# One kernel for attention and two expert layers: GpSimd's work in the seven-product stage given to VectorE, the cosine's argument folded once, half of the cosines computed in the output stage

## The chip, the cores and the metric

The kernel runs on one core of a Trainium2 chip. A core has five engines that run their own instruction streams: TensorE (PE, matmuls), VectorE (DVE), ScalarE (ACT), GpSimd (POOL) and SyncE (SP, which here issues the DMAs). The metric is device time of one execution, in microseconds (us); lower is better. The kernel before the change took 1310.09 us, the median of three runs (1306.05 to 1311.13).

## The reference, cut to what matters

Attention over 4 batches, 8 heads, 576 tokens, head size 64, which keeps the 32 largest scores of a row; then a gated layer on the 2304 tokens; then a second layer with a cosine in it, which the change is about.

```python
def _moe_ref(x, w_gate, w_val, w_out):            # 512 -> 1536 -> 512
    g = x @ w_gate
    silu = g * (1.0 / (1.0 + np.exp(-g)))
    return (silu * (x @ w_val) @ w_out)

def _moe2_ref(x, w_in, w_out):                    # 512 -> 2048 -> 512
    h = x @ w_in
    g = h * np.cos(h)
    return (g @ w_out)
```

All inputs and the output are float32. The kernel works in a reduced float32 form of TensorE: where it needs the full precision, an operand is split into a high half (a copy by ACT into the reduced type) and a low half (the difference, a `tensor_sub`), and three matmuls are summed: high by high, low by high, high by low.

## The kernel before, in words

The 2304 tokens are 18 tiles of 128. Attention runs in units of one tile and one head; the first layer runs beside it in ten chunks (`SIZES`, two chunks of one tile and eight of two). `gemm_proc` computes gate and value of a chunk, 12 steps of 128 hidden columns; `wout_proc` multiplies by the output weights; `y_proc` turns the result and stores it to DRAM (`y1`). The last chunk comes when attention is done: its PSUM banks are three of a new pool (`psB`, banks 0 to 2), and its gated product (`silu`, `product`, L937 and L940) and its low half (L966) are made by DVE.

The second layer's first matmul (hidden 2048) is computed in Strassen's manner, seven products in place of eight. It has 4 groups of 576 tokens (`NCB`) and, for each, 8 pairs of 128-column hidden blocks (`NPR`), in all 32 pairs; a pair makes two rows, of 128 x 576. For each token group `x2_proc` loads four blocks of `y1`, forms four differences (POOL, L1352) and splits the seven operands into high half (ACT, L1369) and low half (DVE, L1373). For each two pairs `win_proc` does the same with the weights, once: four sums and differences (POOL, L1268), seven high halves (ACT, L1284), seven low halves (L1288, DVE for five, POOL for two). A weight set goes into tiles that the last chunk's weights have left; the last of its four sets waits for that chunk's end. `h_proc` runs a pair: seven steps of six matmuls (L1402) on three PSUM banks, between them three copies to SBUF by ACT (L1433, L1489 and one more) and four additions or copies from PSUM by DVE (L1446, L1467, L1474, L1480), on which the next steps wait. The first `ALONE` pairs use banks 3, 4 and 5 one after the other, the next ones up to `BOTH` alternate between banks 0 to 2 and 3 to 5, later ones go around all eight.

`row_proc` takes each of the 64 rows h. It divides by two pi and rounds to a whole number of turns (ACT, L1538, into int32), subtracts the turns from h in two steps with a two-part constant (DVE, L1545 and L1549), takes the absolute value and the sine (ACT, L1552, L1554), multiplies by h (POOL, L1555) and stores the row to DRAM (`gd`). A ring of three tiles holds the rows of either side until then.

The output stage (`piece_proc`, `o_proc`) loads `gd` in 72 pieces of 128 tokens x 512 hidden columns (tile t, quarter m of 4), splits each into halves (ACT L1626, DVE L1630) and runs 12 matmuls per piece (L1653). `wout2_proc` prepares the 16 weight tiles (ACT L1584, POOL L1587). The first four tiles go quarter by quarter (`AHEAD`), the others tile by tile. A loaded piece is in one of five tiles (tag xr), a split one in one of seven (tag xc), which the last pair's operands share.

The order of the instructions on each engine is fixed when the program is built: every step is a generator's item with an engine, a cost and a due time, and `Plan.run` gives each engine, as it comes free, the ready item with the earliest due time. At run time an engine executes its list strictly in order and waits on semaphores. Three lines show the form of an item:

```python
yield "DVE", 0.67, rest, due, True                  # engine, cost in us, what to issue, due time, depends
item = min((x for x in queue if x[0] <= t), key=lambda x: x[1:3])
self.free[engine] = end
```

Of the kernel before, what the change touches and what calls it, by code (L numbers as in the profile page):

```python
# [40 lines left out]
CB = S  # L41
NCB = NTOK // CB
NLAST = 3
ALONE = 3
BOTH = 6
AHEAD = 4
WLEAD = 20.0
HALF = S // 2
SCALE = 1.0 / math.sqrt(D)
STEEP = 2.0 ** 96  # L50
LOWEST = -3.0e38
INV2PI = 1.0 / (2.0 * math.pi)
C1 = 6.28125
C2 = 2.0 * math.pi - C1
SIGN = -2 ** 31
NK = 10
NQ = 3
# [108 lines left out]
def topk_attention_moe_moe(ctx: ExitStack, tc: tile.TileContext, qT, kT, vP, w1, wo1, w2, out):  # L166
# [672 lines left out]
    r_y = [Ring(1) for _ in range(NYB)]  # L839
    ev_g = {(c, f): Event() for c in range(NCH) for f in range(NF1)}  # L840
    ev_gemm = {(c, f): Event() for c in range(NCH) for f in range(NF1)}
    ev_tanh = Event()
    r_o = [Ring(1) for _ in range(4)]
    steps = [NF1 // 2 if turned else NF1 for turned in TURNED]
    K0 = [sum(steps[:c]) for c in range(NCH + 1)]
# [41 lines left out]
    def gemm_proc(c, f):  # L887
# [5 lines left out]
        yield ev_w1[f]  # L893
        last = c == NCH - 1
        if last:
            yield ev_pb
        n = SIZES[c] * 128
        gv, done = {}, [Event(), Event()]

# [26 lines left out]
        if last:  # L926
            done[1].set(end + plan.LAT["PE"], plan)
            yield done[0]
            yield done[1]
            yield r_vv.gate(k)  # L930
            th = TH.pop(k)
            if f == NF1 - 1:
                ev_tanh.set(done[0].time, plan)

            def silu():
                VV[k] = wide("vv", n)
                nc.vector.scalar_tensor_tensor(VV[k], th, 1.0, gv[0], op0=OP.add, op1=OP.mult)  # L937

            def product():
                nc.vector.scalar_tensor_tensor(VV[k], VV[k], 0.5, gv[1], op0=OP.mult, op1=OP.mult)  # L940

            end = yield "DVE", 0.36, silu, due, True
            rings[0][0].free(rings[0][1], end, plan)
            r_th.free(k, end, plan)
            end = yield "DVE", 0.36, product, due, True
            rings[1][0].free(rings[1][1], end, plan)
            vv = VV[k]
        else:
            for g in range(2):
# [13 lines left out]

        yield "ACT", 0.07 + 0.00092 * n, hi, due, True
        eng, name, cost = (nc.vector, "DVE", 0.33) if last else (nc.gpsimd, "POOL", 0.05 + 0.0025 * n)
        end = yield name, cost, lambda: eng.tensor_sub(G[c, f][1], vv, G[c, f][0]), due, True  # L966
        r_vv.free(k, end, plan)
        ev_g[c, f].set(end, plan)

# [115 lines left out]
            r_x.free(2 + c, end, plan)  # L1085

    def y_proc(c, i):
        due = moe_due(c, NF1)
        bank = yt[i % NYB]
        y4 = bank.rearrange("p (f n) -> p f n", f=KT)  # L1090
        for half in range(2):
            ko = yo_count[0]
            yo_count[0] += 1
            yield r_yo.gate(ko)
            y2 = y4[:, 2 * half:2 * half + 2]
            st = {}
# [25 lines left out]
    HN = CB // 2  # L1122
    NPR = NF2 // 2
    SEVEN = 7
    ev_pb, ev_pbx, ev_ph = Event(), Event(), Event()
    X2, W2I, W2O = {}, {}, {}
    ev_w2 = {(q, m): Event() for q in range(NF2 // 4) for m in range(SEVEN)}
    ev_x2 = {(j, m): Event() for j in range(NCB) for m in range(SEVEN)}
# [1 line left out]
    ev_gd = [Event(NF2) for _ in range(NCB)]  # L1130
    r_xc, r_wr, r_xr = Ring(SEVEN), Ring(5), Ring(5)
    r_ha, r_hb2, r_k2, r_r2 = Ring(3), Ring(3), Ring(2), Ring(4)
    ev_rows = {n: Event() for n in range(NCB * NF2)}
# [15 lines left out]
    def pool_b_proc():  # L1149
# [7 lines left out]
            opened("psB", space=PSUM, side="right", reuse_waits="tile")  # L1157

        t = yield "-", 0.0, swap, 0.0, True
        ev_pb.set(t, plan)  # L1160
        for f in range(NF1):
            yield ev_gemm[NCH - 1, f]
# [61 lines left out]
    def win_proc(q):  # L1224
# [32 lines left out]
        def add(m, x, y, op, first, wait=()):  # L1257
            yield have[x]
            yield have[y]
            for e in wait:  # L1260
                yield e

            def fn():
                if m == "S3":
                    alloc(m)
                else:
                    tiles[m] = tiles[first]
                nc.gpsimd.tensor_tensor(tiles[m], tiles[x], tiles[y], op=op)  # L1268

            t = yield "POOL", 1.3, fn, due + W_ORDER.index(m), True  # L1270
            made(m, t)
            done(x, t)
            done(y, t)

        def split(n, m):
# [8 lines left out]
                nc.scalar.activation(w[:, 0], tiles[m], AF.Copy)  # L1284

            yield "ACT", 0.52, hi, d, True
            eng, name, cost = (nc.gpsimd, "POOL", 1.25) if n % 3 == 2 else (nc.vector, "DVE", 0.75)
            t = yield name, cost, lambda: eng.tensor_sub(W2I[q, n][:, 1], tiles[m], W2I[q, n][:, 0]), d, True  # L1288
            done(m, t)
            ev_w2[q, n].set(t, plan)  # L1290

# [17 lines left out]
    def x2_proc(j):  # L1309
# [29 lines left out]
        def add(m, x, y, first, wait=()):  # L1339
# [7 lines left out]
            def fn():  # L1347
                if m in ("T1", "T2"):
                    alloc(m)
                else:  # L1350
                    tiles[m] = tiles[first]
                nc.gpsimd.tensor_sub(tiles[m], tiles[x], tiles[y])  # L1352

            t = yield "POOL", 1.5, fn, due - 12.0, True
            have[m].set(t, plan)
            done(x, t)
            done(y, t)
# [1 line left out]
        def split(n, m):  # L1359
# [7 lines left out]
            def hi():  # L1367
# [2 lines left out]

            t = yield "ACT", 0.6, hi, due + n * 0.5, True
            ev_xh[j, n].set(t, plan)
            t = yield ("DVE", 0.8, lambda: nc.vector.tensor_sub(X2[j, n][:, 1], tiles[m], X2[j, n][:, 0]),  # L1373
                       due + n * 0.5, True)
            done(m, t)
            ev_x2[j, n].set(t, plan)
# [143 lines left out]
    r_s1, r_s2, r_s3 = Ring(2), Ring(1), Ring(1)  # L1520
    ev_wfree = {(q, n): Event() for q in range(NF2 // 4) for n in range(SEVEN)}

    def row_proc(k, side, rows, ready):
        n = 2 * k + side
        j, f = divmod(n, NF2)
        due = b_due(k) + 8.0 + side
        yield ready
        if n:
            yield ev_rows[n - 1]
        yield ev_pbx  # L1530
        yield r_k2.gate(n)
        yield r_r2.gate(n)
        h = rows[side]
        st = {}

        def turns():
            st["k"] = pools["pbx"].tile([128, CB], I32, tag="k", name="k", bufs=r_k2.n)
            nc.scalar.activation(st["k"], h, AF.Copy, scale=INV2PI)  # L1538

        t = yield "ACT", 0.6, turns, due, True  # L1540
        ev_rows[n].set(t, plan)

        def rest():
            r = st["r"] = pools["pbx"].tile([128, CB], F32, tag="r", name="r", bufs=r_r2.n)
            nc.vector.scalar_tensor_tensor(r, st["k"], -C1, h, op0=OP.mult, op1=OP.add)  # L1545

        yield "DVE", 0.67, rest, due, True
        r = st["r"]
        t = yield ("DVE", 0.67, lambda: nc.vector.scalar_tensor_tensor(r, st["k"], -C2, r, op0=OP.mult, op1=OP.add),  # L1549
                   due, True)  # L1550
        r_k2.free(n, t, plan)
        yield "ACT", 0.6, lambda: nc.scalar.activation(r, r, AF.Abs), due, True  # L1552
        yield ev_tanh
        yield "ACT", 0.6, lambda: nc.scalar.activation(r, r, AF.Sin, scale=-1.0, bias=halfpi), due, True  # L1554
        t = yield "POOL", 1.5, lambda: nc.gpsimd.tensor_mul(r, r, h), due, True  # L1555
        (r_ha, r_hb2)[side].free(k, t, plan)
        t = yield "DMA", 1.2, lambda: nc.sync.dma_start(gd[:, f, j * CB:j * CB + CB], r), due, True
        r_r2.free(n, t, plan)
        ev_gd[j].set(t, plan)

    def o_due(n):
# [2 lines left out]
    def wout2_proc(f):  # L1564
# [19 lines left out]
            nc.scalar.activation(W2O[f][:, 0], st["x"], AF.Copy)  # L1584

        yield "ACT", 0.52, hi, due + 3.0, True
        t = yield ("POOL", 1.25, lambda: nc.gpsimd.tensor_sub(W2O[f][:, 1], st["x"], W2O[f][:, 0]), due + 3.0, True)  # L1587
        r_wr.free(i, t, plan)
        ev_w2o[f].set(t, plan)

# [10 lines left out]
    def piece_proc(t, m):  # L1601
# [14 lines left out]

        end = yield "DMA", 1.2, load, due - 6.0, True
        ev_gt[n].set(end - 2.0, plan)
        if n:
            yield ev_gh2[n - 1]  # L1620
        yield r_xc.gate(SEVEN * NCB + n)

        def hi():
            GP[n] = pools["pb"].tile([128, 2, 2, HN], F32R, tag="xc", name="gp", bufs=r_xc.n).rearrange(
                "p a b c -> p a (b c)")[:, :, :DM]
            nc.scalar.activation(GP[n][:, 0], st["x"], AF.Copy)  # L1626

        end = yield "ACT", 0.52, hi, due, True
        ev_gh2[n].set(end, plan)
        end = yield "DVE", 0.75, lambda: nc.vector.tensor_sub(GP[n][:, 1], st["x"], GP[n][:, 0]), due, True  # L1630
        r_xr.free(6 * NCB + n, end, plan)
        ev_gp[n].set(end, plan)

# [119 lines left out]
```

## Time and profile before

| | us |
|---|---|
| median of three runs | 1310.09 |
| profiled execution | 1312.63 |
| its span | 1310.9 |
| PE busy | 1210.4 (92%) |
| DVE busy | 1055.0 (80%) |
| ACT busy | 926.7 (71%) |
| POOL busy | 771.0 (59%) |

The span runs from the first to the last instruction; the execution's own time is 1.7 us more. The slices below divide it into 40 equal parts of 32.8 us; a digit is the busy share in tenths, and PEclk is TensorE's granted clock in tenths of full speed.

```
PE   6799989999999999999999997987878788999998
DVE  7999999999999999989999927479998989522220
POOL 5898957776877677777767555246555577200000
PEclk9799999999999999999999999988989999999999
```

Attention fills the first 24 slices, the last chunk and the seven-product stage the next ten, the output stage the rest.

### The profile page before, as it was taken

How to read it: one execution, taken by the hardware profiler on the slowest of the kernel's cores; microseconds unless marked ns; L12 is line 12 of the kernel's file. 1: busy time of each engine (PE TensorE's matmuls, PEld its weight loads, DVE VectorE, ACT ScalarE, POOL GpSimd, SP SyncE). 2: the span in 40 equal slices, each digit the busy share in tenths (PEclk: the TensorE clock that was granted, in tenths of full speed). 3: DMA queues.
4: the chain of work that ended last, by engine and by line, in shares of the span. 5: the costliest groups of instructions: out<-in, count | busy, mean ns of one | idle time of the engine just before them, and what ended most of it. 6: DMA issues, size and time to landing. Idle time of an engine off the chain costs nothing. (4 is left out here: it accounts for less than half of the span.)

```text
span 1310.9 us, 23535 instructions
## 1 busy us (share of the span) xinstructions
PE 1210.4 (92%) x7720; PEld 1040.0 (79%) x7720; DVE 1055.0 (80%) x1920; ACT 926.7 (71%) x2073; POOL 771.0 (59%) x1156
## 2 busy tenths in 40 slices
PE   6799989999999999999999997987878788999998
PEld 3577647898988988888989887877878787888887
DVE  7999999999999999989999927479998989522220
ACT  4789988988888898988978754267766767422221
POOL 5898957776877677777767555246555577200000
PEclk9799999999999999999999999988989999999999
DMA  7545556665546545565453335532323263643340
GB/s 242 188 148 179 177 167 200 218 198 172 188 145 200 184 157 180 176 202 193 150 187 125 112 98 158 171 100 81 110 82 109 87 199 127 185 130 118 115 121 25
DMA packets 138987, 199.98 MB, mean 153 GB/s; under 512 B 19312, under 2 KB 88432, under 8 KB 138864
## 3 DMA queue, kind: packets, MB, share of 16 engines
q1 hardware_dynamic: 138704, 198.40, 47.8%
q8 instruction: 61, 1.00, 0.3%
q14 instruction: 62, 0.51, 0.1%
q10 hardware_dynamic: 160, 0.07, 0.0%
HBM read 152.28 MB, written 46.14 MB: 151 GB/s over the span
## 5 line engine op out<-in xcount | busy, mean ns | idle before, releaser
L628 DVE MAX8 m<-w 128x8 f32<-128x576 f32 x432 | 311.0, 748 | 1.8
L903 PE MATMUL gv<-x,w 128*128 128x256 f32 x2016 | 283.6, 288 | 1.9 <-ACT hg L870 1.7
L903 PEld LDWEIGHTS gv<-x,w 128*128 128x128 f32 x2016 | 259.0, 190 | 8.8 <-ACT hg L870 3.0
L1402 PE MATMUL b<-xc,w 128*128 128x288 f32 x1344 | 209.7, 315 | 44.3 <-DVE h L1467 21.7
L1402 PEld LDWEIGHTS b<-xc,w 128*128 128x128 f32 x1344 | 195.8, 202 | 57.0 <-DVE h L1467 26.3
L631 DVE MATCH_REPLACE8 w<-m,w 128x576 f32<-128x576 f32 x288 | 213.3, 742 | 0.0
L1653 PE MATMUL b<-w2o,gp 128*128 128x512 f32 x864 | 201.8, 396 | 0.0
L1653 PEld LDWEIGHTS b<-w2o,gp 128*128 128x128 f32 x864 | 162.3, 188 | 39.2
L1067 PE MATMUL y<-wo,gh 128*128 128x512 f32 x400 | 148.8, 414 | 7.7 <-DMA wo<-wo 5.1
L1555 POOL TENSOR_TENSOR r<-r,h 128x576 f32<-128x576 f32 x64 | 105.6, 1654 | 84.4 <-ACT r L1554 50.1
L1630 DVE TENSOR_TENSOR gp<-gr,gp 128x512 fp32r<-128x512 f32 x72 | 54.2, 760 | 121.7 <-ACT gp L1626 121.7
L628 DVE MAX8 m<-s 128x8 f32<-128x576 f32 x144 | 107.7, 748 | 16.0 <-ACT s L603 13.9
L659 ACT ACTIVATE e<-s,b 128x576 f32<-128x576 f32 x144 | 114.1, 794 | 8.2 <-POOL b L642 8.1
L670 ACT ACTIVATE e<-e,b 128x576 f32<-128x576 f32 x144 | 114.5, 795 | 2.8 <-POOL b L646 0.3
L603 ACT ACTIVATE s<-sc 128x576 f32<-128x576 f32 x144 | 95.5, 663 | 20.4 <-PE sc L591 15.6
L631 DVE MATCH_REPLACE8 w<-m,s 128x576 f32<-128x576 f32 x144 | 106.9, 742 | 0.0
L698 ACT ACTIVATE pt<-tp 128x512 f32<-128x512 f32 (+1 forms) x216 | 101.5, 501 | 4.6 <-PE tp L692 3.3
L1626 ACT ACTIVATE gp<-gr 128x512 fp32r<-128x512 f32 x72 | 44.8, 627 | 84.4 <-PE b L1653 78.7
L692 PE MATMUL tp<-ident,e 128*128 128x128 f32 x648 | 99.4, 278 | 4.8 <-ACT pt L698 2.3
L1067 PEld LDWEIGHTS y<-wo,gh 128*128 128x128 f32 x400 | 75.1, 189 | 30.6 <-issue 7.0
L598 PE MATMUL sc<-K,q 128*128 128x288 f32 (+1 forms) x512 | 91.2, 304 | 2.9 <-ACT s L603 2.6
L1545 DVE SCALAR_TENSOR_TENSOR r<-k,h 128x576 f32<-128x576 int32 x64 | 79.6, 1249 | 14.7 <-ACT k L1538 14.2
(112 smaller groups left out, 2363.7 us busy)
## 6 DMA issues: line engine op xcount, KB each, us to landing
wo<-wo SPq DMA_DIRECT2D x96, 512.0 KB, 3.6
gd<-r SPq DMA_DIRECT2D x64, 288.0 KB, 2.1
gr<-gd SPq DMA_DIRECT2D x72, 256.0 KB, 2.9
w_raw<-in_w SPq DMA_DIRECT2D x32, 511.8 KB, 4.2
V<-in_vP SPq DMA_DIRECT2D x52, 256.0 KB, 3.0
w<-in_w SPq DMA_DIRECT2D x24, 511.5 KB, 5.9
kx<-in_kT SPq DMA_DIRECT2D x64, 144.0 KB, 3.3
wo<-wo SPq DMA_DIRECT2D x36, 256.0 KB, 2.9
```

Of the source, the lines that this page charges most:

```text
L603: nc.scalar.activation(st["s"], sc[:, :, :HALF], AF.Copy)
L628: nc.vector.max(out=st["m"][:, 8 * i:8 * i + 8], in_=st["w"] if i else st["s"])
L631: nc.vector.match_replace(out=st["w"], in_to_replace=st["m"][:, 8 * i:8 * i + 8], in_values=st["w"] if i else st["s"], imm_value=LOWEST)
L659: nc.scalar.activation(st["e"], st["s"], AF.Prelu, bias=st["b"][:, 1:2], scale=SCALE, alpha=STEEP)
L670: nc.scalar.activation(st["e"], st["e"], AF.Exp, bias=st["b"][:, 2:3], scale=1.0, accum_out=smT[c, p, g][:, j:j + 1])
L692: nc.tensor.transpose(st["ps"][:, j - j0], e[:, j * 128:j * 128 + 128], ident)
L698: nc.scalar.activation(pt[:, j0:j1], st["ps"][:, :j1 - j0], AF.Copy)
L903: nc.tensor.matmul(gv[g], W1[f, kk // 2][:, a, g, kk % 2], m, start=kk == 0 and i == 0, stop=kk == KT - 1 and i == 2)
L1067: nc.tensor.matmul(bank, m, w, start=f == 0 and n == 0, stop=f == NF1 - 1 and n == len(terms) - 1)
L1402: nc.tensor.matmul(ps[b], w[:, a, side, kk], x[:, e, kk], start=start and kk == 0 and m == 0, stop=kk == 1 and m == 2, skip_group_check=True)
L1555: t = yield "POOL", 1.5, lambda: nc.gpsimd.tensor_mul(r, r, h), due, True
L1653: nc.tensor.matmul(st["o"], g[:, a, cs], W2O[f][:, b], start=f == 0 and i == 0, stop=f == NF2 - 1 and i == 2)
```

## The change

- `ALONE` is 1 instead of 3.
- In the last chunk the items of `silu`, `product` and the low half get due times 80 us earlier, as do the items of `y_proc` for the last two chunks. The chunk waits for an event of its own (`ev_psb`), set at the same place as `ev_pb`.
- All POOL items behind the attention go to DVE: sums and differences of weights and x, the remaining low halves of weights, the low halves of the output weights, the product of cosine and h. Costs given to the planner change with them.
- The turns are subtracted in one step, on h / (2 pi), and the sine's scale is -2 pi instead of -1.
- Rows of hidden blocks 4 to 7 and 12 to 15 (`LATE`, quarters 1 and 3) are stored as h, without a cosine. Their cosine is computed in `piece_proc`, on the loaded piece of 128 x 512, before it is split.

```diff
-ALONE = 3
+ALONE = 1
+LATE = (1, 3)
...
-            end = yield "DVE", 0.36, silu, due, True
+            end = yield "DVE", 0.36, silu, due - 80.0, True
...
-        end = yield name, cost, lambda: eng.tensor_sub(G[c, f][1], vv, G[c, f][0]), due, True
+        end = yield name, cost, lambda: eng.tensor_sub(G[c, f][1], vv, G[c, f][0]), due - 80.0 * last, True
...
-        due = moe_due(c, NF1)
+        due = moe_due(c, NF1) - 80.0 * (c >= NCH - 2)
...
-                nc.gpsimd.tensor_tensor(tiles[m], tiles[x], tiles[y], op=op)
-            t = yield "POOL", 1.3, fn, due + W_ORDER.index(m), True
+                nc.vector.tensor_tensor(tiles[m], tiles[x], tiles[y], op=op)
+            t = yield "DVE", 0.62, fn, due + W_ORDER.index(m), True
...
-            eng, name, cost = (nc.gpsimd, "POOL", 1.25) if n % 3 == 2 else (nc.vector, "DVE", 0.75)
-            t = yield name, cost, lambda: eng.tensor_sub(W2I[q, n][:, 1], tiles[m], W2I[q, n][:, 0]), d, True
+            t = yield "DVE", 0.62, lambda: nc.vector.tensor_sub(W2I[q, n][:, 1], tiles[m], W2I[q, n][:, 0]), d, True
...
-                nc.gpsimd.tensor_sub(tiles[m], tiles[x], tiles[y])
-            t = yield "POOL", 1.5, fn, due - 12.0, True
+                nc.vector.tensor_sub(tiles[m], tiles[x], tiles[y])
+            t = yield "DVE", 0.67, fn, due - 12.0, True
...
+    early = [n for n in range(NCB * NF2) if n % NF2 // 4 not in LATE]
+    turn_of = {n: i for i, n in enumerate(early)}
+
+    def cosine(i, h, width, due):
+        if i:
+            yield ev_rows[i - 1]
+        yield ev_pbx
+        yield r_k2.gate(i)
+        yield r_r2.gate(i)
+        st = {}
+
+        def turns():
+            st["k"] = pools["pbx"].tile([128, CB], I32, tag="k", name="k", bufs=r_k2.n)[:, :width]
+            nc.scalar.activation(st["k"], h, AF.Copy, scale=INV2PI)
+
+        per = width / CB
+        t = yield "ACT", 0.6 * per, turns, due, True
+        ev_rows[i].set(t, plan)
+
+        def rest():
+            st["r"] = pools["pbx"].tile([128, CB], F32, tag="r", name="r", bufs=r_r2.n)[:, :width]
+            nc.vector.scalar_tensor_tensor(st["r"], h, INV2PI, st["k"], op0=OP.mult, op1=OP.subtract)
+
+        t = yield "DVE", 0.67 * per, rest, due, True
+        r = st["r"]
+        r_k2.free(i, t, plan)
+        yield "ACT", 0.6 * per, lambda: nc.scalar.activation(r, r, AF.Abs), due, True
+        yield ev_tanh
+        yield ("ACT", 0.68 * per,
+               lambda: nc.scalar.activation(r, r, AF.Sin, scale=-2.0 * math.pi, bias=halfpi), due, True)
+        t = yield "DVE", 0.67 * per, lambda: nc.vector.tensor_mul(r, r, h), due, True
+        return r, t
...
+        if n in turn_of:
+            r, t = yield from cosine(turn_of[n], h, CB, due)
+            ring.free(k, t, plan)
+        else:
+            r = h
         t = yield "DMA", 1.2, lambda: nc.sync.dma_start(gd[:, f, j * CB:j * CB + CB], r), due, True
...
-        t = yield ("POOL", 1.25, lambda: nc.gpsimd.tensor_sub(W2O[f][:, 1], st["x"], W2O[f][:, 0]), due + 3.0, True)
+        t = yield ("DVE", 0.62, lambda: nc.vector.tensor_sub(W2O[f][:, 1], st["x"], W2O[f][:, 0]), due + 3.0, True)
...
+        x = st["x"]
+        if m in LATE:
+            i = len(early) + len(LATE) * t + LATE.index(m) if t >= AHEAD else len(early) + LATE.index(m) * AHEAD + t
+            x, end = yield from cosine(i, st["x"], DM, due)
...
-        end = yield "DVE", 0.75, lambda: nc.vector.tensor_sub(GP[n][:, 1], st["x"], GP[n][:, 0]), due, True
+        end = yield "DVE", 0.62, lambda: nc.vector.tensor_sub(GP[n][:, 1], x, GP[n][:, 0]), due, True
+        if m in LATE:
+            r_r2.free(i, end, plan)
```

## Rows read from the trace of the kernel before

**Rows 1.** Stretches: us, busy us of PE, PEld, DVE, ACT, POOL, clock, DMA, GB/s
```profile
785.00:856.00 71.00, 62.72 (x413) 56.95 (x412) 39.40 (x55) 24.89 (x58) 31.71 (x22) 0.95 0.53 171
856.00:1105.00 249.00, 203.64 (x1317) 190.75 (x1316) 222.78 (x277) 176.19 (x335) 151.85 (x94) 0.92 0.32 108
1105.00:1311.00 206.00, 202.24 (x869) 162.62 (x868) 62.30 (x81) 60.79 (x102) 13.52 (x8) 1.00 0.39 118
```

**Rows 2.** Chain that ended last: start us, us, engine, line, count
```profile
1105.64 201.61 PE b L1653 x864
```

**Rows 3.** DVE's groups, 856 to 1105: busy us, mean ns; idle before
```profile
L1545 DVE SCALAR_TENSOR_TENSOR r<-k,h 128x576 f32<-128x576 int32 x60 | 73.5, 1229 | 14.7 <-ACT k L1538 14.2 <-issue 0.5
L1549 DVE SCALAR_TENSOR_TENSOR r<-k,r 128x576 f32<-128x576 int32 x60 | 72.2, 1205 | 0.6
L1373 DVE TENSOR_TENSOR xc<-xr,xc 128x576 fp32r<-128x576 f32 x21 | 25.6, 1250 | 0.1
...
L1288 DVE TENSOR_TENSOR w<-wr,w 128x512 fp32r<-128x512 f32 x10 | 10.8, 1114 | 1.5 <-ACT w L1284 1.5
```

**Rows 4.** Timeline of DVE: start us, us, line, operation [idle before]
```profile
907.11 1.86 DVE L1549 SCALAR_TENSOR_TENSOR r<-k,r 128x576 f32<-128x576 int32 x1
...
911.08 0.68 DVE L1288 TENSOR_TENSOR w<-wr,w 128x512 fp32r<-128x512 f32 x1
912.58 0.46 DVE L1446 TENSOR_TENSOR h<-b,s 128x288 f32<-128x288 f32 x1 [0.82 <-PE b L1402]
912.95 0.75 DVE L1545 SCALAR_TENSOR_TENSOR r<-k,h 128x576 f32<-128x576 int32 x1
913.62 0.45 DVE L1474 TENSOR_TENSOR h<-b,s 128x288 f32<-128x288 f32 x1
```

**Rows 5.** Timeline of POOL beside it
```profile
906.42 3.83 POOL L1555 TENSOR_TENSOR r<-r,h 128x576 f32<-128x576 f32 x2
911.56 1.50 POOL L1555 TENSOR_TENSOR r<-r,h 128x576 f32<-128x576 f32 x1 [1.31 <-ACT r L1554]
```

**Rows 6.** Timeline of DVE in the output stage, POOL idle
```profile
1131.41 0.69 DVE L1630 TENSOR_TENSOR gp<-gr,gp 128x512 fp32r<-128x512 f32 x1 [3.55 <-ACT gp L1626]
```

**Rows 7.** Parts of the last chunk's stretch, columns as in rows 1
```profile
800.00:823.00 23.00, 16.36 (x82) 13.90 (x83) 19.52 (x19) 10.15 (x23) 15.84 (x10) 0.85 0.30 95
823.00:856.00 33.00, 31.55 (x214) 28.71 (x213) 14.82 (x26) 9.10 (x22) 10.81 (x8) 1.00 0.60 196
```

**Rows 8.** Timeline of DVE in the last chunk
```profile
802.79 5.30 DVE L1288 TENSOR_TENSOR w<-wr,w 128x512 fp32r<-128x512 f32 x3
```

**Rows 9.** Timeline of PE in the last chunk
```profile
813.74 1.93 PE L903 MATMUL gvl<-x,w 128*128 128x256 f32 x12 [3.37 <-DVE vv L940]
```

**Rows 10.** PE's groups, 856 to 1105 us
```profile
L1402 PE MATMUL b<-xc,w 128*128 128x288 f32 x1299 | 201.5, 315 | 43.0 <-DVE h L1467 21.7 <-ACT s L1433 6.6 <-ACT s L1489 5.1
```

**Rows 11.** Timeline of ACT in the seven-product stage
```profile
999.95 0.76 ACT L1554 ACTIVATE r<-r,halfpi 128x576 f32<-128x576 f32 x1
1000.62 0.67 ACT L1538 ACTIVATE k<-h 128x576 int32<-128x576 f32 x1
1001.19 0.40 ACT L1433 ACTIVATE s<-b 128x288 f32<-128x288 f32 x1
1001.48 0.68 ACT L1552 ACTIVATE r<-r 128x576 f32<-128x576 f32 x1
```

**Rows 12.** Timeline of PE at the start of the 31 pairs
```profile
856.23 4.17 PE L1402 MATMUL b<-xc,w 128*128 128x288 f32 x30
860.24 0.39 PE L1067 MATMUL y<-wo,gh 128*128 128x512 f32 x1
```

**Rows 13.** DMA issues: count, KB each, median us to landing
```profile
gr<-gd SPq DMA_DIRECT2D x72, 256.0 KB, 2.9
```

**Rows 14.** Waits in the output stage: us in total, times, longest
```profile
ACT gp L1626 <- PE b L1653: 78.7, 40, 2.2
```

**Rows 15.** POOL's waits, 856 to 1105 us
```profile
POOL r L1555 <- ACT r L1554: 46.2, 25, 5.8
```

More of the change, by code (lines that the diff above doesn't have):

```diff
@@ L52 @@
 INV2PI = 1.0 / (2.0 * math.pi)
-C1 = 6.28125
-C2 = 2.0 * math.pi - C1
 SIGN = -2 ** 31
@@ L841, in topk_attention_moe_moe @@
     ev_gemm = {(c, f): Event() for c in range(NCH) for f in range(NF1)}
-    ev_tanh = Event()
+    ev_tanh, ev_pb, ev_psb = Event(), Event(), Event()
     r_o = [Ring(1) for _ in range(4)]
@@ L895, in gemm_proc @@
         if last:
-            yield ev_pb
+            yield ev_psb
         n = SIZES[c] * 128
@@ L940, in product @@
                 nc.vector.scalar_tensor_tensor(VV[k], VV[k], 0.5, gv[1], op0=OP.mult, op1=OP.mult)
-            end = yield "DVE", 0.36, silu, due, True
+            end = yield "DVE", 0.36, silu, due - 80.0, True
             rings[0][0].free(rings[0][1], end, plan)
             r_th.free(k, end, plan)
-            end = yield "DVE", 0.36, product, due, True
+            end = yield "DVE", 0.36, product, due - 80.0, True
             rings[1][0].free(rings[1][1], end, plan)
@@ L1124, in topk_attention_moe_moe @@
     SEVEN = 7
-    ev_pb, ev_pbx, ev_ph = Event(), Event(), Event()
+    ev_pbx, ev_ph = Event(), Event()
     X2, W2I, W2O = {}, {}, {}
@@ L1132, in topk_attention_moe_moe @@
     r_ha, r_hb2, r_k2, r_r2 = Ring(3), Ring(3), Ring(2), Ring(4)
-    ev_rows = {n: Event() for n in range(NCB * NF2)}
+    ev_rows = {n: Event() for n in range(2 * NCB * NF2)}
     ev_mm = {(k, m): Event() for k in range(NCB * NPR) for m in range(SEVEN)}
@@ L1159, in pool_b_proc @@
         t = yield "-", 0.0, swap, 0.0, True
+        ev_psb.set(t, plan)
         ev_pb.set(t, plan)
@@ L1372, in split @@
             ev_xh[j, n].set(t, plan)
-            t = yield ("DVE", 0.8, lambda: nc.vector.tensor_sub(X2[j, n][:, 1], tiles[m], X2[j, n][:, 0]),
+            t = yield ("DVE", 0.67, lambda: nc.vector.tensor_sub(X2[j, n][:, 1], tiles[m], X2[j, n][:, 0]),
                        due + n * 0.5, True)
@@ L1527, in row_proc @@
         yield ready
[L1528 to L1532, printed above, removed]
-        h = rows[side]
[L1534 to L1556, printed above, removed]
+        h = rows[side]
+        ring = (r_ha, r_hb2)[side]
+        if n in turn_of:
[3 more added lines that the diff above has]
+            r = h
         t = yield "DMA", 1.2, lambda: nc.sync.dma_start(gd[:, f, j * CB:j * CB + CB], r), due, True
-        r_r2.free(n, t, plan)
+        if n in turn_of:
+            r_r2.free(turn_of[n], t, plan)
+        else:
+            ring.free(k, t, plan)
         ev_gd[j].set(t, plan)
@@ L1625, in hi @@
                 "p a b c -> p a (b c)")[:, :, :DM]
-            nc.scalar.activation(GP[n][:, 0], st["x"], AF.Copy)
+            nc.scalar.activation(GP[n][:, 0], x, AF.Copy)
         end = yield "ACT", 0.52, hi, due, True
         ev_gh2[n].set(end, plan)
-        end = yield "DVE", 0.75, lambda: nc.vector.tensor_sub(GP[n][:, 1], st["x"], GP[n][:, 0]), due, True
+        end = yield "DVE", 0.62, lambda: nc.vector.tensor_sub(GP[n][:, 1], x, GP[n][:, 0]), due, True
+        if m in LATE:
+            r_r2.free(i, end, plan)
         r_xr.free(6 * NCB + n, end, plan)
```

## The prediction

> **What bounds the kernel now.** I read the page's slices first, then busy time by stage, then the chain of waits, then the vector engine's (DVE's) groups and single instructions. The slices show TensorE (PE) at nine tenths or more up to the 24th of 40, seven or eight in most of the next ten, nine again behind them. Three stretches follow: the last chunk of the first expert layer (785 to 856 us), the seven-product stage (856 to 1105) and the output stage (1105 to the end) [rows 1]. In the third PE is busy 202 of 206 us; the chain there is one run of 864 matmuls, 201.61 us, and no wait [rows 2]. Nothing that prepares its operands costs time there. In the second PE works 203.6 of 249 us at a granted clock of 0.92, while DVE is busy 222.8 us, nine tenths, more than any other engine. So the seven-product stage is set by DVE, and a gain has to be looked for there.
>
> What DVE does there is in its groups [rows 3]: two folds of the cosine's argument for each row of products, 73.5 and 72.2 us, 1.23 and 1.21 us each, and the low halves of the operands, 1.25 and 1.11 us each. These are not the instructions' own times. The same fold took 1.86 us at 907.11 while GpSimd (POOL) ran, and held DVE only 0.67 us at 912.95 (start of the next less its own) [rows 4], where POOL's only instruction was at its end [rows 5]. In the output stage, where POOL has stopped, a low half of 512 columns takes 0.69 us [rows 6]. An addition that reads one operand from PSUM took 0.46 us and held DVE 0.37 us at 912.58, while POOL's product ran [rows 4, 5]. So it is instructions with two operands in SBUF that POOL stretches, and POOL is busy 152 of these 249 us [rows 1].
>
> The Trainium skill's page "SBUF — State Buffer", section "Who interferes with whom", says that a DVE instruction with two SBUF inputs and a GpSimd instruction that reads SBUF hold a shared port in turn, whole instructions at a time, and that one with a single SBUF input does not contend. The trace agrees: 1.86 us against 0.75 us for the fold, 0.46 us for the addition from PSUM with POOL at work.
>
> **The last chunk.** From 800 to 823 us PE has 82 matmuls in 23 us at a clock of 0.85; in the 33 us behind it, 214 [rows 7], 6.5 to the microsecond. At that rate 82 take 12.7 us: 10.3 us are lost. The reason is six low halves on DVE, two runs of three, 5.3 us each, in front of the chunk's own two-step product (silu, product) [rows 8], for which PE then waited 3.37 us [rows 9]. The change puts the chunk's DVE work 80 us ahead in due time, and POOL stretches nothing any more. DVE does get eleven W and eleven x instructions for the first pair: 11 x 0.61 + 11 x 0.67 = 14 us, in a stretch of 71 us where it was busy 39.4, much of it stretched. A silu can now wait behind one instruction of 0.67 us, not three. I take 8 of the 10.3 us; bounds 4 and 10.3. The chunk ends at 848 instead of 856.
>
> "Only one pair ahead" costs nothing, I think: of the stage's 1344 matmuls 1299 lie between 856 and 1105 [rows 10] and a few behind, so some 40 before 856, and one pair has 42: it is one already. What differs is which banks pairs 1 and 2 use: 0 to 2 and 3 to 5 in turn, instead of 3 to 5 for both. Banks 0 to 2 come free with the chunk's last product, where pair 1 started anyway. If that hands back late, one evacuation, 0.45 us.
>
> **The seven-product stage, 31 pairs.** DVE by parts, alone on its port (0.67 us for 576 columns, 0.69 - 0.08 = 0.61 for 512, 0.37 from PSUM):
> - four additions a pair: 124 x 0.37 = 45.9 us, as now
> - early rows: 32 of 64; one fold each instead of two, and the product with h, which was POOL's: 64 x 0.67 = 42.9
> - x operands of three token groups, 4 differences (POOL's before) and 7 low halves: 33 x 0.67 = 22.1
> - W operands, three sets of 11 at most: 33 x 0.61 = 20.1
> - output weights, 16 low halves (POOL's before): 9.8
>
> That is 140.8 us instead of 222.8. ScalarE (ACT) loses half of the cosines: starts to starts, 0.57 for the turns, 0.58 for the absolute value, 0.67 for the sine, 0.29 for a PSUM copy [rows 11]; 31 pairs with three copies and one cosine make 31 x (0.87 + 1.82) = 83 us, and some 25 to 35 us of high halves: about 115 us. Neither is the bound.
>
> PE then is. From 856.23 thirty matmuls ran up to 860.24 [rows 12]: 0.134 us each, 5.6 us for a pair's 42, 173.6 us for 31 pairs at full clock. Two and a half us of transposes and products left by the chunk lie among them. Bounds: no wait left, 5.6 a pair; or all of the 43.0 us that PE idles on these matmuls now [rows 10] stays, at full clock: 216.6 us, 7.0 a pair. I choose nearer the first, since 21.7 of the 43 us end on one DVE addition, and the share that ends on ACT's copies (11.7 us of the 43) is what has no reason to go: 11.7 / 31 = 0.4, so 6.0 us a pair, 186 us. The low clock went with PE's gaps (0.85 where it worked 16.36 of 23 us, 1.00 where it worked almost without gaps [rows 7]); with few gaps I count it as full.
>
> W operands: the last of the fourth set left DVE at 911.08 [rows 4], 55 us behind the chunk's end, and pairs 6 and 7 need it. With additions that follow each other in 0.61 us rather than queue behind POOL's other work, I let it be ready before pair 6, 30 us behind the chunk. Price if not: the third rival.
>
> **The output stage.** 36 of 72 pieces get a cosine of 512 columns. ACT: three more, at most 1.82 us each piece; DVE: two more, 1.22. For an early and a late piece together PE takes 2 x 201.61 / 72 = 5.6 us; ACT some 2 x 0.55 + 1.82 = 2.9 and half an evacuation, DVE 3 x 0.61 + 0.61 = 2.4. So there is room by two. What would be late is the first late piece, the fifth in order; four early pieces, 11.2 us of PE, stand before it, and its chain is load 2.9 [rows 13], then 0.57 + 0.67 + 0.58 + 0.67 + 0.61 + 0.55 + 0.61 = 4.3 us. The cover is that pieces run ahead: ACT waits 78.7 us in total for PE to give tiles back [rows 14]. I count 0; bounds 0 and, for a start that is late by one chain, 7 us. The stored rows move nothing on the DMA queue: 64 stores and 72 loads as before; half of the stores leave a cosine earlier.
>
> **Sum.** In the profiled execution's time: 848 + 186 + 2.4 + 205.3 (from the first output matmul to the end) = 1241.7 of span, plus 1.7 outside it (1312.6 against 1310.9) = 1243.4. The median of the runs lies 2.5 below that execution, so 1241 us. Own range: chunk end 845.7 and 5.6 a pair give 1226; 852 and 7.0 a pair give 1276.
>
> **Rivals.**
> 1. DVE's instructions stay as long as they are today: then it is not POOL that stretches them. For: the means of 1.1 to 1.25 us hold over the whole stage. Against: rows 4 and 6. By today's means the stage loses 145.7 us of folds, gains 64 x 1.23 = 79 for early rows, 10 x 1.25 + 11 x 1.11 for differences, sums and halves of x and W, 14 x 1.11 for output weights = 40: net 26 us, nothing at the chunk: 1284 us. The skill's "Perfetto Trace Analysis", section "Optimizing Scalar/DVE Operations", has the rule against this change, to offload a saturated DVE to ScalarE or GpSimd; it adds that between DVE and GpSimd this might not help. By the rule's first half, this rival; by its second, the forecast.
> 2. DVE now stands where POOL stood. POOL waited 46.2 us for the sine [rows 15]; DVE takes its instructions in order, and behind a waiting product stand the additions that PE waits for. The early rows are 32 of the 59 in that stretch, so 25 us; all of it passed on to PE: 1266. Against: DVE has 45 us to spare in 186.
> 3. The W sets stay 55 us behind the chunk: pair 6 starts at 903 instead of 848 + 2.4 + 30 = 880: 23 us, 1264. This is also how the change would fail to do what it says: DVE freed, PE still waiting.
> 4. Slower: in the output stage a late piece holds its loaded tile from load to low half, and with five such tiles loads no longer run ahead. An early and a late piece then take 2.9 + 4.3 + 1.2 = 8.4 us, 2.8 more than PE's 5.6; over 36 such couples 101 us, 1342. It decides as soon as a couple takes more than 5.6 us, and turns the sign above 7.5 a couple (70 us lost). Against: ACT's wait of 78.7 us, and 2.9 and 2.4 us of work per couple.
>
> **How the numbers follow.** Forecast 0.76, rivals 0.07, 0.08, 0.05, 0.04. The first three rivals are all faster than before by over 0.5% (6.5 us, about what a measurement of this kernel can tell from no change): faster 0.94. Same 0.02 is taken from rival 1 with a late start of the output stage on top, slower 0.04 is rival 4. The range reaches from just below the forecast's lower end (5.6 us a pair still holds a little filling of the pipeline) to just above its upper one, and so over rivals 2 and 3: 1223 to 1278. Outside lie rivals 1 and 4 and some tail of the rest.
>
> **What the new profile would show.** POOL empty behind the attention's last chunk. Folds, low halves and products on DVE at 0.67 to 0.75 us throughout. The first output matmul near 1036. PE in the stage busier than nine tenths, DVE about three quarters, clock near 1.00. The run of 864 output matmuls unbroken at about 202 us. The prediction is wrong if DVE's two-operand instructions still take over 1 us (rival 1), if PE's idle time ends on DVE instructions that themselves wait for ACT (rival 2), on a W low half (rival 3), or if gaps open among the output matmuls (rival 4).

## The result, and the profile after

The changed kernel takes 1238.22 us (median of four runs, 1237.47 to 1239.47) against 1310.61 beside it: a ratio of 0.9453, 95% interval 0.9427 to 0.9479. The forecast was 1241, from 1223 to 1278. Most of its steps held; one, on the pairs ahead of the last chunk, did not, and with it what was said of the chunk's due times; both are shown below.

Busy time by stretch of the changed kernel first: last chunk, seven-product stage up to the first output matmul, output stage; columns as in [rows 1].

```profile
786.95:847.12 60.17, 58.49 (x412) 54.58 (x411) 36.58 (x73) 25.72 (x58) 1.95 (x3) 1.00 0.63 204
847.12:1030.73 183.61, 177.46 (x1307) 175.75 (x1306) 137.85 (x254) 127.25 (x249) 0.00 (x0) 0.99 0.44 149
1030.73:1234.10 203.37, 203.37 (x878) 163.73 (x876) 99.06 (x150) 118.19 (x199) 0.00 (x0) 1.00 0.39 115
```

Cut at the same marks, the trace before has 70.9, 249.4 and 201.8 us. So 10.7 us went in the chunk, 65.8 in the stage, and the output stage shows 1.6 more, because twelve matmuls of the last pair now run behind its first one. The chunk's start is no mark: over the runs told here its first matmul lies between 780.8 and 789.7 us, though the work ahead of it is the same. Lengths of stretches are compared below, not times of day.

In the stage DVE has gone from 223.3 to 137.9 us, POOL from 152.3 to 0, and PE from 82% to 97% busy, the clock from 0.92 to 0.99. The slices of the changed kernel's page (32.8 us each before, 30.9 now):

```profile
PE   6699988999999999999999999998999999999998
...
DVE  6999999999999999998999996267867778544441
...
POOL 4898976777677776776777765300000000000000
PEclk9899989999999999999999999999999999999999
```

PE is at nine tenths or more in every slice from the eighth on, but for one and the last. Its own timeline in the stage says what is left: two waits on one DVE addition each of 3.20 and 1.34 us, two smaller ones, and then one run of 1080 matmuls.

```profile
853.10 4.38 PE L1401 MATMUL b<-xc,w 128*128 128x288 f32 x30
...
860.99 3.25 PE L1401 MATMUL b<-xc,w 128*128 128x288 f32 x12 [3.20 <-DVE h L1466]
...
881.34 2.67 PE L1401 MATMUL b<-xc,w 128*128 128x288 f32 x18 [1.34 <-DVE h L1466]
885.02 1.05 PE L1401 MATMUL b<-xc,w 128*128 128x288 f32 x6 [1.02 <-DVE h L1466]
886.63 144.27 PE L1401 MATMUL b<-xc,w 128*128 128x288 f32 x1080 [0.55 <-DVE h L1479]
1030.73 1.56 PE L1672 MATMUL b<-w2o,gp 128*128 128x512 f32 x6
```

144.27 us for 1080 are 0.1336 us each, the 0.134 of [rows 12]: 5.6 us a pair, with nothing in between. In front of the first of these additions DVE works through the third weight set:

```profile
858.68 1.89 DVE L1287 TENSOR_TENSOR w<-wr,w 128x512 fp32r<-128x512 f32 x3
860.48 0.45 DVE L1466 TENSOR_TENSOR h<-b,s 128x288 f32<-128x288 f32 x1
```

DVE's groups there answer to [rows 3]; columns as there.

```profile
L1552 DVE TENSOR_TENSOR r<-r,h 128x576 f32<-128x576 f32 x32 | 24.2, 755 | 7.7 <-ACT r L1551 7.7
L1543 DVE SCALAR_TENSOR_TENSOR r<-h,k 128x576 f32<-128x576 f32 x32 | 23.9, 750 | 0.1
...
L1372 DVE TENSOR_TENSOR xc<-xr,xc 128x576 fp32r<-128x576 f32 x21 | 15.3, 751 | 0.7 <-ACT xc L1368 0.6
L1466 DVE TENSOR_TENSOR h<-b,s 128x288 f32<-128x288 f32 x31 | 14.1, 456 | 9.8 <-PE b L1401 9.7
...
L1287 DVE TENSOR_TENSOR w<-wr,w 128x512 fp32r<-128x512 f32 x14 | 9.1, 685 | 0.0
```

The fold takes 750 ns where it took 1229 (and there is one for 32 rows instead of two for 64), the low half of x 751 where it took 1250, that of the weights 685 where it took 1114. The addition from PSUM, 456 ns, is what it was (446). In the output stage no wait stands in front of an output matmul: its group has 0.0 us of idle time over 864 matmuls.

### The profile page after: what moved, and what is told of

It reads as the page before. It is cut to its first block, busy times and chain, and to the rows that moved or that the text cites. A ratio compares the mean times of both kernels' runs of the same rounds, so it can differ in the third digit from the quotient of the medians.

```text
span 1237.7 us, 23277 instructions
## 1 busy us (share of the span) xinstructions
PE 1179.8 (95%) x7720; PEld 1021.3 (83%) x7720; DVE 1003.4 (81%) x1984; ACT 936.6 (76%) x2085; POOL 575.6 (47%) x1036
## 4 chain that ended last, share of the span: by engine, by line
PE 56%; DMA 7%; ACT 7%; DVE 4%; POOL 4%; issue 2%; SPq 0%; POOLq 0%; ACTq 0%; DVEq 0%
PE b L1672 16%; PE b L1401 13%; PE gv L902 10%; PE y L1066 7%; PE av L747 3%; PE sc L597 2%; PE gvl L902 2%; PE tp L691 2%; DMA kx<-in_kT 2%; DVE m L627 1%; DVE w L630 1%; DMA w2d<-w_raw 1%; DMA wo<-wo 1%; DMA qx<-in_qT 1%; DMA w_raw<-in_w 1%
## 5 line engine op out<-in xcount | busy, mean ns | idle before, releaser
L1401 PE MATMUL b<-xc,w 128*128 128x288 f32 x1344 | 184.2, 298 | 6.1 <-DVE h L1466 5.6
L1401 PEld LDWEIGHTS b<-xc,w 128*128 128x128 f32 x1344 | 181.5, 189 | 7.6 <-DVE h L1466 6.3
L691 PEld LDWEIGHTS tp<-ident,e 128*128 128x128 f32 x648 | 77.9, 142 | 16.9 <-ACT pt L697 6.7
L1066 PE MATMUL y<-wo,gl 128*128 128x512 f32 x208 | 85.6, 418 | 6.1 <-POOL gl L965 3.0
L965 POOL TENSOR_TENSOR gl<-vv,gh 128x256 fp32r<-128x256 f32 x84 | 62.0, 738 | 42.5 <-ACT gh L961 29.0
L597 PEld LDWEIGHTS sc<-K,q 128*128 128x128 f32 (+1 forms) x512 | 73.4, 184 | 8.3 <-ACT s L602 3.7
```

The source lines that it names most:

```text
L597: nc.tensor.matmul(sc[:r1, s, :HALF], q[:, a, (t - t0) * 128:(t - t0) * 128 + r1], k[:, s * HALF:s * HALF + HALF], start=a == 0, stop=a == 1)
L691: nc.tensor.transpose(st["ps"][:, j - j0], e[:, j * 128:j * 128 + 128], ident)
L1066: nc.tensor.matmul(bank, m, w, start=f == 0 and n == 0, stop=f == NF1 - 1 and n == len(terms) - 1)
L1401: nc.tensor.matmul(ps[b], w[:, a, side, kk], x[:, e, kk], start=start and kk == 0 and m == 0, stop=kk == 1 and m == 2, skip_group_check=True)
```

## The experiments

All times are medians, with the ratio to the kernel before, which ran beside each (1309.3 to 1311.5 us). Lengths are those of the profiled execution: chunk, then stage up to the first output matmul. That execution can lie some us from the median, furthest with the chunk's edits undone (1252.4 against 1245.3).

| kernel | us | ratio, interval | chunk | stage |
|---|---|---|---|---|
| before | 1310.6 | 1 | 70.9 | 249.4 |
| changed | 1238.2 | 0.9453 (0.9427 to 0.9479) | 60.2 | 183.6 |
| POOL's work moved, alone | 1269.2 | 0.9689 (0.9657 to 0.9722) | 73.3 | 199.5 |
| one fold, alone | 1281.5 | 0.9782 (0.9758 to 0.9805) | 69.1 | 218.6 |
| late rows, alone | 1270.2 | 0.9695 (0.9666 to 0.9725) | 69.0 | 204.2 |
| changed, no late rows | 1245.1 | 0.9502 (0.9476 to 0.9528) | 61.2 | 193.0 |
| changed, two folds | 1244.9 | 0.9514 (0.9470 to 0.9558) | 60.1 | 188.7 |
| changed, POOL kept | 1264.1 | 0.9650 (0.9601 to 0.9700) | 71.0 | 201.4 |
| changed, chunk's edits undone | 1245.3 | 0.9517 (0.9472 to 0.9561) | 74.8 | 179.2 |
| changed, three pairs ahead | 1247.3 | 0.9521 (0.9495 to 0.9548) | 61.0 | 194.0 |
| changed, idle products on POOL | 1285.6 | 0.9816 (0.9781 to 0.9851) | 84.6 | 209.6 |
| changed, idle memsets on POOL | 1237.5 | 0.9452 (0.9414 to 0.9489) | 60.8 | 183.7 |
| changed, two weight sets yield | 1240.7 | 0.9455 (0.9430 to 0.9479) | 60.0 | 185.1 |
| changed, one weight set yields | 1238.7 | 0.9455 (0.9433 to 0.9477) | 61.4 | 183.8 |

Two of the chunks (POOL's work moved alone; the chunk's edits undone) hold 30 more matmuls of the pairs, 4.0 us that the stage then lacks.

### POOL's work moved to DVE, alone

```diff
-                nc.gpsimd.tensor_sub(tiles[m], tiles[x], tiles[y])
-            t = yield "POOL", 1.5, fn, due - 12.0, True
+                nc.vector.tensor_sub(tiles[m], tiles[x], tiles[y])
+            t = yield "DVE", 0.67, fn, due - 12.0, True
...
-        t = yield "POOL", 1.5, lambda: nc.gpsimd.tensor_mul(r, r, h), due, True
+        t = yield "DVE", 0.67 * per, lambda: nc.vector.tensor_mul(r, r, h), due, True
```

(`per` is 1 for a whole row; and the same for sums of weights, low halves, output weights)

> The kernel before with one part of the change alone: POOL's work behind the attention goes to DVE; two folds, all cosines in the stage, three pairs ahead and the last chunk's due times as before. Theory (DVE's load sets the stage, and the freed port gives back only what the moved work adds): DVE alone on its port carries 45.9 + 64 x 3 x 0.67 + 22.1 + 20.1 + 9.8 = 226 us against 222.8 before, so the stage stays near 240 us and the kernel comes to 1290 to 1308. Rival (POOL's use of the port is the whole of the loss): most of the 72 us comes with this part, 1250 to 1265.

Measured: 1269.2 us, between the two ranges and nearer the rival's. DVE's groups in its stage, in the same form as above:

```profile
L1545 DVE SCALAR_TENSOR_TENSOR r<-k,h 128x576 f32<-128x576 int32 x59 | 44.3, 757 | 0.0
L1550 DVE SCALAR_TENSOR_TENSOR r<-k,r 128x576 f32<-128x576 int32 x58 | 43.8, 756 | 0.2
L1556 DVE TENSOR_TENSOR r<-r,h 128x576 f32<-128x576 f32 x57 | 43.0, 757 | 1.3 <-ACT r L1555 1.3
```

With two folds and 57 products besides, DVE is busy 193.9 us of 199.5: the bound still, with hardly a gap. The theory's load was right in kind and misplaced: 226 us counts all the work of 31 pairs, but part of the weights' work falls into the chunk and the tail of the rows into the output stage. Over the three stretches together DVE's busy time fell from 324.5 us (39.4, 223.3, 61.8) to 306.4 (44.5, 193.9, 68.0) while it took on nearly all that had kept POOL busy 197 us (31.5, 152.3, 13.0). The freed port gave back more than the moved work adds.

### One fold, alone, and late rows, alone

```diff
-            nc.vector.scalar_tensor_tensor(r, st["k"], -C1, h, op0=OP.mult, op1=OP.add)
...
-        t = yield ("DVE", 0.67, lambda: nc.vector.scalar_tensor_tensor(r, st["k"], -C2, r, op0=OP.mult, op1=OP.add),
+            nc.vector.scalar_tensor_tensor(st["r"], h, INV2PI, st["k"], op0=OP.mult, op1=OP.subtract)
```

> The kernel before with the fold of the cosine's argument in one instruction instead of two, POOL's work left on POOL. Theory (DVE's load): DVE loses one 1.2 us instruction for each of 64 rows, 77 us, and comes to some 150 to 165 us in the stage, under PE's 174; kernel 1250 to 1275. Rival (the port): instructions beside POOL stay at 1.2 us or grow, gain under 25 us, 1285 to 1300.

> The kernel before with the cosines of half of the rows moved to the output stage, two folds each, products on POOL. Theory (DVE's load): the stage loses 64 folds of 1.2 us on DVE and 32 products on POOL, DVE some 145 us, PE sets the pace: 1240 to 1265; the output stage stays at 202 us. Rival (late pieces hold the output matmuls, since the product of a piece now takes 1.3 to 1.7 us on POOL): gaps among the 864 output matmuls, over 1270.

(The second adds `LATE = (1, 3)` and the cosine in `piece_proc` to the kernel before.) Measured: 1281.5 and 1270.2. DVE's load came out about as expected, 161.3 us of 218.6 and 150.3 of 204.2, but the times lie 6.5 and 5.2 us above the ends of the theory's ranges: with POOL still at work DVE is no longer full, and PE still waits for it. The second time is also just over the rival's 1270 us, though not by the rival's gaps, as the end of this part shows. The waits of PE in the stage of the one-fold kernel (us in total, times, longest):

```profile
PE b L1402 <- DVE h L1467: 17.2, 11, 6.4
PE b L1402 <- DVE xc L1373: 5.3, 3, 3.0
```

and what ACT waits for there:

```profile
ACT r L1549 <- DVE r L1544: 21.3, 16, 4.6
ACT r L1549 <- POOL r L1553: 8.4, 9, 1.2
```

A fold takes up to 2.0 us there and holds what stands behind it in DVE's list, and engines that wait for one another's results pass the delay on: the wait of 6.4 us ends on an addition that stands behind three low halves of weights, 5.26 us together. These kernels, like the one with POOL's work moved alone, also keep three pairs ahead, which costs 9 us in the changed kernel (below); how much of the two misses comes from that was not run. In the late-rows kernel the output matmuls waited once, 1.7 us, for the low half of the first late piece. That is the late start for which the forecast had left up to 7 us, and not rival 4, in which every late piece would hold the loads up.

### Parts of the change undone

```diff
-LATE = (1, 3)
+LATE = ()
```

> The changed kernel with all cosines in the seven-product stage (no row left for the output stage). Theory (load): DVE 140.8 + 32 x 1.34 = 184 us and ACT about 175 us against PE's 174, so DVE just sets the stage, 8 to 20 us longer: 1246 to 1260. Rival (after the port is free DVE has room enough): 1238 to 1242.

Measured: 1245.1 us, 6.8 more; chunk and stage together 10.4 more, with DVE at 170.4 of 193.0 us and ACT at 172.6. Load theory, just below the low end of its range.

```diff
-            nc.vector.scalar_tensor_tensor(st["r"], h, INV2PI, st["k"], op0=OP.mult, op1=OP.subtract)
+            nc.vector.scalar_tensor_tensor(st["r"], st["k"], -C1, h, op0=OP.mult, op1=OP.add)
...
+                   lambda: nc.vector.scalar_tensor_tensor(r, st["k"], -C2, r, op0=OP.mult, op1=OP.add), due, True)
```

> The changed kernel with the argument folded in two instructions again. Theory (load): DVE 140.8 + 32 x 0.67 = 162 us, still under PE's 174: 1238 to 1246. Rival (every instruction on DVE counts): 21 us more on the path, 1255 to 1260.

Measured: 1244.9, stage 5.1 us longer. As expected: 18 us more on DVE in the stage (155.7 against 137.9) cost 5.

```diff
-        t = yield "DVE", 0.67 * per, lambda: nc.vector.tensor_mul(r, r, h), due, True
+        t = yield "POOL", 1.5 * per, lambda: nc.gpsimd.tensor_mul(r, r, h), due, True
```

(and the other POOL items of before, with the costs of before)

> The changed kernel with POOL's work left on POOL (sums and differences, some low halves, the product with h). Theory (load): DVE does 124 additions of 0.37 us and some 73 two-operand instructions stretched to about 1.2 us, 135 us, under PE's 174: 1240 to 1262. Rival (POOL's leaving is what makes the gain): 1280 or more.

Measured: 1264.1, 26 us more, just above the theory's end. Of chunk and stage 28.6 us came back: 10.8 in the chunk, all that the change had gained there, and 17.8 in the stage, where DVE is busy only 128 us of 201. So POOL costs here not by DVE's load but by the length of single instructions in front of the additions. Of PE's 14.9 us of waits in this stage (6.2 in the changed kernel) 12.3 end on additions; besides, PE is busy 185.8 us instead of 177.5, at a granted clock of 0.97 instead of 0.99. Two such waits on PE's timeline, and DVE's beside them:

```profile
894.85 1.52 PE L1402 MATMUL b<-xc,w 128*128 128x288 f32 x6 [4.43 <-DVE h L1467]
898.43 10.25 PE L1402 MATMUL b<-xc,w 128*128 128x288 f32 x62 [2.06 <-DVE h L1480]
```

```profile
889.94 4.48 DVE L1288 TENSOR_TENSOR w<-wr,w 128x512 fp32r<-128x512 f32 x3
894.35 0.45 DVE L1467 TENSOR_TENSOR h<-b,s 128x288 f32<-128x288 f32 x1
894.71 3.20 DVE L1544 SCALAR_TENSOR_TENSOR r<-h,k 128x576 f32<-128x576 f32 x2
897.83 0.45 DVE L1480 COPY h<-b 128x288 f32<-128x288 f32 x1
```

Three low halves of weights and two folds, 1.5 and 1.6 us each, stand in front of the additions.

### The port by itself

POOL gets work that nobody waits for, on a tile of its own.

```diff
+    def idle_proc():
+        yield ev_pbx
...
+        for i in range(120):
+            yield "POOL", 1.3, lambda: nc.gpsimd.tensor_mul(z, z, z), 0.0, True
```

> The changed kernel with 120 products of 128 x 512 on POOL from the end of the last chunk on, which read and write one tile that nothing else uses. Theory (two-operand instructions of DVE and POOL's reads exclude each other): DVE's folds, products and low halves grow from 0.75 to 1.1 to 1.4 us while POOL runs, its additions from PSUM stay at 0.45, DVE is the bound again: 1260 to 1300. Rival (the stretch before came from somewhere else): 1238 to 1242.

The other kernel has 290 times `nc.gpsimd.memset(z, 0.0)` in its place.

> The changed kernel with 290 memsets of 128 x 512 on POOL from the end of the last chunk on, which write one tile that nothing else uses and read nothing. If POOL's reads are what stretches DVE: DVE's two-operand instructions stay at 0.75 us, 1238 to 1241. If any access of POOL to SBUF does: 1255 to 1300, as with products.

Measured: 1285.6 and 1237.5. POOL began both earlier than the texts say, within the chunk, since its list held nothing else. With products, DVE and POOL side by side:

```profile
875.63 2.97 DVE L1287 TENSOR_TENSOR w<-wr,w 128x512 fp32r<-128x512 f32 x2
878.52 1.52 DVE L1268 TENSOR_TENSOR wr<-wr 128x512 f32<-128x512 f32 x1
879.97 1.52 DVE L1287 TENSOR_TENSOR w<-wr,w 128x512 fp32r<-128x512 f32 x1
881.41 1.52 DVE L1268 TENSOR_TENSOR wr<-wr 128x512 f32<-128x512 f32 x1
```

```profile
869.82 15.46 POOL L1732 TENSOR_TENSOR idle<-idle 128x512 f32<-128x512 f32 x11
```

Eleven products took 15.46 us, 1.41 each, and DVE's weight items, 0.68 us in the changed kernel, come every 1.45 us: about one DVE instruction for each of POOL's. With memsets the groups of the same lines are those of the changed kernel:

```profile
L1552 DVE TENSOR_TENSOR r<-r,h 128x576 f32<-128x576 f32 x28 | 21.2, 757 | 7.1 <-ACT r L1551 7.1
L1543 DVE SCALAR_TENSOR_TENSOR r<-h,k 128x576 f32<-128x576 f32 x28 | 20.9, 750 | 0.0
...
L1466 DVE TENSOR_TENSOR h<-b,s 128x288 f32<-128x288 f32 x27 | 12.3, 455 | 9.7 <-PE b L1401 9.7
...
L1287 DVE TENSOR_TENSOR w<-wr,w 128x512 fp32r<-128x512 f32 x14 | 9.1, 685 | 0.0
```

```profile
L1732 POOL MEMSET idle<- 128x512 f32 x191 | 100.7, 527 | 11.0
```

POOL was busy 100.7 us here and nothing became longer. In the kernel with products, PE waited 22.9 us in five waits for one addition, the longest 9.1, and the chunk took 84.6 us; from 987 us, with POOL done, PE was busy 88.0 of 88.0 us. This is the cause of the long instructions before, shown by itself: POOL's instructions that read SBUF, beside DVE's with two operands there. It is also what "SBUF — State Buffer" of the Trainium skill states in "Who interferes with whom", that a DVE instruction with two SBUF inputs contends with a GpSimd instruction that reads SBUF and not with one that only writes; its exemption for a single SBUF input, which the prediction gives without a condition, holds there outside the two-port modes.

### The last chunk

```diff
-ALONE = 1
+ALONE = 3
...
-            end = yield "DVE", 0.36, silu, due - 80.0, True
+            end = yield "DVE", 0.36, silu, due, True
```

(and the other due times of the chunk and of the stores behind it)

> The changed kernel with three pairs ahead and the due times of the last chunk and its stores as before. Theory: the chunk ends some 4 to 8 us later behind low halves of 0.6 us, 1241 to 1248. Rival (both edits do nothing once DVE is quick): 1238.

> The changed kernel with three pairs ahead of the last chunk, all else as changed. With both edits of the last chunk undone, chunk and stage together took 254.0 us against 243.8, and the chunk held 30 more matmuls of later pairs. Theory (the due times are what counts, the pairs ahead only move matmuls from one side of the chunk's end to the other): 1236 to 1241. Rival (the pairs ahead stand in PE's list before the chunk's own products and hold it): 1242 to 1247.

Measured: 1245.3 with both undone, in the theory's range, and 1247.3 with `ALONE = 3` alone. The second is the rival's time by another mechanism: the chunk is as short as in the changed kernel (61.0 us, no more matmuls in it), and the stage is 10.4 us longer. A part of PE's timeline at its start, in the kernel with three pairs ahead:

```profile
853.43 1.04 PE L1401 MATMUL b<-xc,w 128*128 128x288 f32 x6
857.48 0.64 PE L1105 MATMUL y<-ident,yo 128*128 128x128 f32 x2 [3.00 <-ACT yo L1099]
861.13 1.81 PE L1401 MATMUL b<-xc,w 128*128 128x288 f32 x6 [3.00 <-DVE h L1466]
862.74 0.63 PE L1105 MATMUL y<-ident,yo 128*128 128x128 f32 x2
863.49 5.38 PE L1401 MATMUL b<-xc,w 128*128 128x288 f32 x24
```

and the same stretch by tens, columns as in [rows 1]:

```profile
847.00:857.00 10.00, 6.80 (x46) 6.08 (x44) 6.51 (x12) 9.14 (x18) 0.00 (x0) 1.00 0.12 43
857.00:867.00 10.00, 6.39 (x24) 5.58 (x25) 7.45 (x14) 6.46 (x15) 0.00 (x0) 0.53 0.35 108
...
877.00:887.00 10.00, 6.62 (x37) 6.39 (x36) 6.86 (x13) 3.11 (x7) 0.00 (x0) 0.72 0.15 58
```

Pairs 1 and 2 share three banks there, so PE has six matmuls of pairs at hand at 853.43 where the changed kernel runs 30 from 853.10. It then waits twice: 3.00 us for a copy of the chunk's result (`yo`), which stands behind high halves of weights in ACT's list, and 3.00 us for the addition behind the third weight set, the one wait that the changed kernel has here. Its granted clock is 0.53 in the ten us from 857 (0.83 in the changed kernel), half speed for nearly all of them, and six matmuls take 1.81 us where six at 853.43 took 1.04. With both edits undone the three pairs run partly inside the chunk, which is longer by as much: chunk and stage make 254.0 and 255.0 us, 243.8 in the changed kernel. Earlier due times without the other banks gain nothing; whether the banks alone would was not run.

### The last waits

```diff
-            t = yield "DVE", 0.62, fn, due + W_ORDER.index(m), True
+            t = yield "DVE", 0.62, fn, due + W_ORDER.index(m) + (30.0 if q > 1 else 0.0), True
```

(the low halves likewise; in the second kernel `q == 2` for `q > 1`)

> The changed kernel with the DVE items of the third and fourth weight set due 30 us later, so that they stand behind the additions that PE waits for. The changed kernel's trace has PE idle 3.2, 1.3, 1.0 and 0.6 us between 857 and 887 us, behind runs of weight items on DVE, and a low clock behind the first. Theory (these runs are the last loss of the stage): 1230 to 1235. Rival (the sets then come late for their own pairs): 1236 to 1245.

> The changed kernel with only the third weight set due 30 us later on DVE. With the third and the fourth delayed the wait of 3.2 us behind the third set went, and one of 3.85 us came behind the fourth. Theory (each set makes the wait that its own place makes): the 3.2 us and the low clock behind them go, 1231 to 1236. Rival (a set that yields only moves the wait to the next): 1237 to 1242.

Measured: 1240.7 and 1238.7, no gain. The first is its rival's time, but no wait of PE ends on a weight tile there; its longest, 3.85 us, ends on an addition again. PE's waits for that addition in the second kernel, then in the changed one:

```profile
PE b L1401 <- DVE h L1466: 4.0, 2, 3.8
```

```profile
PE b L1401 <- DVE h L1466: 5.6, 3, 3.2
```

The wait of 3.2 us behind the third set went, and one of 3.8 came behind the fourth: the rival. Why the fourth set's eleven items then come in one block is open. No version here beats the changed kernel.

## Why the prediction was right, and the step that was wrong

- **DVE sets the stage, PE after the change.** Right. 140.8 us were worked out for DVE, 137.9 are in the stage; about three quarters of it, as said. That the two agree so well is partly luck: 33 weight items and 16 output weights were counted where 22 and 12 lie in the stage, while an instruction with nothing behind it holds DVE for its whole 0.75 us (576 columns) and not for the 0.67 from start to start.
- **POOL stretches two-operand instructions.** Right, by the two idle kernels; rival 1 is out with folds at 750 ns.
- **6.0 us a pair.** The stage's 183.6 us less 2.4 us of the chunk's rest, for 1290 of 31 pairs' 1302 matmuls, make 5.9. The allowance of 0.4 was near for another reason than the one given: ACT's copies make no wait of the pairs at all now. Of 6.1 us of idle time 4.5 (3.20 and 1.34) stand behind DVE's third and fourth weight set, with a granted clock of 0.83 in the ten us around the first. That is rival 3's place at a fifth of its price, and not its mechanism: the fourth set leaves DVE 34 us behind the chunk (30 were allowed, 55 it was), and PE waits not for a weight tile but for an addition that stands behind the set in DVE's list.
- **The last chunk, 8 of 10.3 us.** 10.7 came, just above the upper bound. The chunk's length takes both edits that the forecast named: 71.0 us with the due times but POOL at work, 70.8 (74.8 less 4.0 of pairs' matmuls) with POOL gone and the due times as before, 61.0 with both and three pairs ahead, 60.2 in the changed kernel. But the kernel's time gains nothing from the due times by themselves (1247.3 with them, 1245.3 without, three pairs ahead in both), since the stage gets longer by as much; a gain of that size came only with the other banks, 7 us for both edits together.
- **"Only one pair ahead" costs nothing.** It cost nothing, but it was put at nothing, and there the reasoning failed: that pair 1 started behind the chunk in either kernel is right, but not that the banks make no difference beyond one evacuation of 0.45 us. They are worth 9 us in the changed kernel (1247.3 against 1238.2). What they would give in the kernel before, where DVE is full, was not run. The sum came out all the same, in part by luck, since the stage was priced from PE's dense rate, with the alternating banks in place, and not from the pace of the old pairs.
- **The output stage, 0.** Right: 203.4 us with twelve matmuls of the pair in it (12 x 0.134 = 1.6), 201.8 without. ACT still waits 28.1 us for PE there (78.7 before [rows 14]), so pieces still run ahead.
- **Rival 2.** DVE does wait for the sine, 7.7 us in 32 products, and no wait of PE comes from it: DVE has 46 us to spare.
- **The parts are not a sum.** Alone they give 41, 29 and 40 us, undone 26, 7 and 7; 72 together. Each takes load or length off the same engine until PE's 174 us is reached, and only the rest counts. In the expectations, not in the forecast, DVE's load was three times taken for the whole story (one fold alone, late rows alone, POOL kept), and the times came out 2 to 7 us above the ranges; the runs with POOL at work show that the length of a single instruction in an ordered list costs as well (17.8 us of stage with DVE 64% busy).

## What to carry to other kernels

Where an engine is full, compare the same instruction's time beside and away from its neighbours' work before counting its instructions: here the cure for a full DVE was to give it more work and its neighbour none. Bound a stage by its next engine (0.134 us x 42 x 31 here), since gains of several edits end there and can't be added. An edit that looks free beside a full engine has to be priced for the kernel in which that engine is no longer full: the banks of the first pairs, put at nothing, are worth 9 us there.

## What the runs showed of the hardware

POOL's 290 memsets of 128 x 512 (527 ns each) left DVE's two-operand instructions at 0.68 to 0.76 us, its 120 products made them 0.90 to 1.47 us in the mean of their groups (866 to 960 us), while DVE's additions with one operand in PSUM stayed at 0.45 to 0.46 us in both. And a wait costs PE more than its length: over the ten us in which two waits of 3.00 us ended, in the kernel with three pairs ahead, the granted clock was 0.53, about half of full speed (of its two levels, the lower, 1.2 GHz), and with one wait of 3.20 us, in the changed kernel, 0.83.
